# Units four to seven load into the weights' staging tiles, the third job's splits move behind unit seven's places, and 32 dummy matmuls go

## The chip, the cores and the metric

The kernel runs on one core of one Trainium2 chip. The metric is the device time of one execution in microseconds (us). The core has five engines that each take their own instructions in order: PE (matmuls and transposes), DVE (elementwise, scans and reductions), ACT (activations and copies), POOL (here the scatters) and SP (here only DMA issues). ACT and POOL issue DMAs too, and an issue stands in the engine's order like any other instruction.

## The reference

Two parts follow each other. A gated scan runs over 4 sequences of 3648 steps with 256 channels: with z the gate's logits and lower bound lb,

```python
sig = 1.0 / (1.0 + np.exp(-f_logit))
f = lb + (1.0 - lb) * sig
h = f[:, t] * h + (1.0 - f[:, t]) * x[:, t]      # for every step t
```

Then each of the 14592 rows of h goes through a mixture of 16 experts: a router gives 4 group logits and 4 x 4 expert logits, the largest of each picks one expert per row, and the row's result is `combined * (relu(h @ w1[e]) @ w2[e])` with w1 256 x 1024, w2 1024 x 256, and `combined` the product of the two softmax weights that were picked. All is in float32.

## The kernel before, in words

**Units.** The rows are taken in units of 512, counted from 0 (units 0 to 28, the last one half full). Unit u's z and x (1 MB together) are loaded into one `zt` tile (p1_load; four buffers). ACT makes the tanh (L195) and two affine steps (L205), which together are the gate f; DVE multiplies by the gate (L241, from unit 10 on L221; in this text "the gate" of the unit) and runs two scans, one per half of the channels (L232). PE transposes h back to rows (L259) and multiplies by the router's weights (L278). ACT copies these (rs, L283), PE transposes them (L291), ACT copies the logits (Lg, L292). DVE's routing of the unit begins with mx (L301, a maximum over Lg) and ends with posi (L398), the place of each row in its expert's list; between them lie PE's counts (L383 to L386) and small steps on DVE. POOL then scatters the unit's rows to these places in DRAM (L361, four scatters per unit). Units 0 to 7 are routed one by one; from unit 8 on two units are routed together (GROUPS).

**Jobs.** While units are still under way, experts whose list has enough rows are begun: job i takes its first rows once the units below EARLY[i][0] are scattered (4, 6, 8, 8, 10, ...), 256 rows for the first four jobs. SP loads the rows (xr, L852) after the last scatter of those units has landed; PE transposes them (L933), ACT and DVE make the operands. Jobs 0 and 1 multiply in float32 (L967, then L1002) and need no split of the weights. From job 2, "the third job", the weights are loaded into staging tiles `st` (eight of 512 KB), ACT casts them to f16 (wh, L878) and DVE makes the remainder (wl, L879), four of each per job; then come three matmuls for each product (L989 to L991, L1019). After the early jobs, sixteen more take the rest of each expert's list.

**What sets the order.** SP goes in the order in which the program is written. On PE, DVE, ACT and POOL a scheduler moves instructions within the dependences and its own estimates; on every engine the order is then fixed. Loads up to unit 11 stand on SP, later ones on ACT (ZX_SP). In before, p1_load of units u+2 and u+3 is called while unit u is worked on (`range(u + AHEAD - 1, u + FAR)`). A load into a `zt` buffer waits for the scans of the unit that had the buffer. Dummy matmuls (keep_warm, L268) run before each raw job's row transposes, 22 each.

Of the kernel before, what the change touches and what calls it, by code (L numbers as in the profile page):

```python
# [10 lines left out]
F32 = mybir.dt.float32  # L11
# [7 lines left out]
P = 128  # L19
# [18 lines left out]
O_BUFS = 5  # L38
X_BUFS = 4
AHEAD = 3  # L40
FAR = 4
BEGIN = 6
MT = -(-max(CAPS) // 128)
QUARTERS = (13, 14, 15)
ZX_SP = 12
# [3 lines left out]
def gated_scan_moe(ctx: ExitStack, tc, zx, lower, wroute, wexp, out, S):  # L49
# [116 lines left out]
        at += g  # L166
    assert at == NU
    last_load = {}

    def p1_load(u):  # L170
        if u >= NU or u in units:
            return
        a, b = unit_range(u)
        w = b - a
        zt = p1.tile([P, 2, KD, UNIT], F32, name="zt", bufs=4)
        src = zx[u * P:(u + 1) * P, :].rearrange("p (s k w) -> p s k w", s=2, k=KD)
        if u == 0:
            for k in range(KD):
                for q in range(2):
                    nc.sync.dma_start(out=zt[:, q, k, 0:w], in_=src[:, q, k, 0:w])  # L180
        elif u == 1:
            for k in range(KD):
                nc.sync.dma_start(out=zt[:, :, k, 0:w], in_=src[:, :, k, 0:w])
        else:
            last_load[u] = (nc.sync if u < ZX_SP else nc.scalar).dma_start(out=zt[:, :, :, 0:w], in_=src[:, :, :, 0:w])
        units[u] = {"z": zt}

    def p1_tanh(u):
        a, b = unit_range(u)
        w = b - a  # L190
        U = units[u]
        U["h"] = p1.tile([P, KD, UNIT], F32, name="h", bufs=3)
        U["f"] = ff = U["z"][:, 0]
        if u > 1:
            nc.scalar.activation(ff[:, :, 0:w], U["z"][:, 0, :, 0:w], AF.Tanh, scale=0.5)  # L195

    def p1_affine(u):
        a, b = unit_range(u)
        w = b - a
        U = units[u]  # L200
        ff = U["f"]
        for k in range(KD):
            if u <= 1:
                nc.scalar.activation(ff[:, k, 0:w], U["z"][:, 0, k, 0:w], AF.Tanh, scale=0.5)
            nc.scalar.activation(ff[:, k, 0:w], ff[:, k, 0:w], AF.Identity, scale=hlf[:, k:k + 1],  # L205
                                 bias=cen[:, k:k + 1])

# [4 lines left out]
    def p1_tb(u, k):  # L212
        a, b = unit_range(u)
        w = b - a
        U = units[u]
        ff = U["f"]
        h = U["h"]
        U["u"] = U["z"][:, 1]
        if (k == 0 or u <= 1) and "gated" not in U:
            ks = slice(k, k + 1) if u <= 1 else slice(0, KD)  # L220
            nc.vector.scalar_tensor_tensor(out=U["u"][:, ks, 0:w], in0=ff[:, ks, 0:w], scalar=1.0,  # L221
                                           in1=U["z"][:, 1, ks, 0:w], op0=ALU.subtract, op1=ALU.mult)
        uu = U["u"]
        cuts = [a] + [c for c in range(0, N, S) if a < c < b] + [b]
        for c0, c1 in zip(cuts[:-1], cuts[1:]):
            if c0 % S == 0:
                init = 0.0
            elif c0 > a:
                init = h[:, k, c0 - a - 1:c0 - a]
            else:  # L230
                init = units[u - 1]["h"][:, k, UNIT - 1:UNIT]
            nc.vector.tensor_tensor_scan(out=h[:, k, c0 - a:c1 - a], data0=ff[:, k, c0 - a:c1 - a],  # L232
                                         data1=uu[:, k, c0 - a:c1 - a], initial=init,
                                         op0=ALU.mult, op1=ALU.subtract)

    def p1_gate(u):
        a, b = unit_range(u)
        w = b - a
        U = units[u]
        U["gated"] = True  # L240
        nc.vector.scalar_tensor_tensor(out=U["z"][:, 1, :, 0:w], in0=U["f"][:, :, 0:w], scalar=1.0,  # L241
                                       in1=U["z"][:, 1, :, 0:w], op0=ALU.subtract, op1=ALU.mult)

    def p1_back(u, i):
        a, b = unit_range(u)
# [40 lines left out]
    def p1_logits(u, Lg, pos):  # L286
        a, b = unit_range(u)
        nt = (b - a) // P
        rs = units[u]["rs"]
        lt = bank("p")  # L290
        nc.tensor.transpose(out=lt[:, 0:32 * nt], in_=rs[0:32 * nt, 0:P], identity=ident[0:32 * nt, 0:32 * nt])  # L291
        nc.scalar.copy(Lg[:, pos:pos + nt, :], lt[:, 0:32 * nt].rearrange("p (t c) -> p t c", c=32)[:, :, 0:20])  # L292

    def route_thunks(G, T, fast=False):
        V = nc.vector
# [97 lines left out]
        def f5():  # L393
# [1 line left out]
            sc = rt.tile([P, T, NE], F32, name="sc", bufs=1)  # L395
            V.tensor_tensor(out=sc, in0=pv[:, 0:T], in1=R["oh16"], op=ALU.mult)
            posi = R["posi"] = rt.tile([P, T], I32, name="posi", bufs=4)
            V.tensor_reduce(out=posi, in_=sc, axis=AX, op=ALU.add)  # L398
            new = state["runoff"] = rt.tile([P, NE], F32, name="runoff")
            nc.scalar.copy(new, pv[:, T])  # L400

# [5 lines left out]
    def p1_thunks(us, groups, parts):  # L407
# [53 lines left out]
        for u in us + [us[-1] + 1]:  # L461
            seq = []
            if u <= FAST:
                put(lambda u=u: [p1_load(v) for v in range(u + AHEAD - 1, u + FAR)])
                ending = u - 1 in ends
                if not ending:
                    put(lambda u=u: p1_ta(u + 1))
# [405 lines left out]
    def job_split(j, i):  # L873
# [2 lines left out]
        j.wh[i] = wp.tile([P, 1024], F16, name=f"wh{i}")  # L876
        j.wl[i] = wp.tile([P, 1024], BF16, name=f"wl{i}")
        nc.scalar.copy(j.wh[i], j.st[i])  # L878
        nc.vector.tensor_tensor(out=j.wl[i], in0=j.st[i], in1=j.wh[i], op=ALU.subtract)  # L879

    def job_xt(j, pi):
        b0, rows = j.pieces[pi]
        ch = max(i for i, (a, _) in enumerate(j.chunks) if a <= b0)
        c0 = b0 - j.chunks[ch][0]
        if j.raw:
            keep_warm(bank("m2"), 22)
            j.xh[ch] = mo.tile([P, 2 * P], F32, name="xh", bufs=X_BUFS)
            j.xl[ch] = mo.tile([P, 2 * P], F32, name="xl", bufs=X_BUFS)
        elif c0 == 0:
# [360 lines left out]
```

## Time and profile before

| | |
|---|---|
| median of 3 runs | 773.15 us (770.84 to 774.26) |
| profiled execution | 771.69 us, of which the span from the first to the last instruction is 769.8 us |
| mean granted PE clock in the span | 0.981 of full speed |
| busy | PE 720.2 us (94%), DVE 537.2 (70%), ACT 453.3 (59%), POOL 296.7 (39%) |

The profiled execution lies 1.46 us under the median. In a timeline a row gives the start, the duration, engine, line, operation and tile (written <- read), and in brackets the engine's idle time just before it with what ended that. "ACTq" and "SPq" are issues of DMAs on that engine's queue; the transfer itself goes on afterwards. Consecutive instructions of one kind make one row (x8 is eight of them).

### The profile page before, as it was taken

To read this page: it belongs to the slowest core of one execution; us is meant where nothing else is said; L and a number is where in the kernel's file an instruction comes from. 1 tells how busy PE (TensorE), PEld (TensorE's weight loads), DVE (VectorE), ACT (ScalarE), POOL (GpSimd) and SP (SyncE) were. 2 spreads that over 40 slices of the span, in tenths; PEclk is the share of its full clock that TensorE was granted. 3 is DMA by queue.
4 is the path that set the end of the run, shared out by engine and by line. 5 is a ranking of instruction groups with operands and counts; after the bars stand their busy time and mean duration, and the time that the engine had idled before them with its cause. 6 is when DMAs were issued, how large, how long until landed. Compare 5 with 4: busy or idle time off the path is not lost.

```text
span 769.8 us, 21533 instructions
## 1 busy us (share of the span) xinstructions
PE 720.2 (94%) x8179; PEld 640.4 (83%) x8179; DVE 537.2 (70%) x1166; ACT 453.3 (59%) x827; POOL 296.7 (39%) x272
## 2 busy tenths in 40 slices
PE   3668798999999999999999999999999999999995
PEld 1456587988888888898999889999999999999895
DVE  6997669999999986687546545453754675667561
ACT  5647768887787865545545444444544565556551
POOL 3653255587765576441221212222222222223232
PEclk9969899999999999999999999999999999999998
DMA  7799689989888866448875662424254455556530
GB/s 279 223 388 347 211 318 319 358 263 306 324 299 270 261 219 192 124 114 245 197 187 151 149 138 83 125 77 128 92 157 110 142 153 154 155 170 194 165 83 29
DMA packets 101961, 152.02 MB, mean 197 GB/s; under 512 B 60962, under 2 KB 70977, under 8 KB 98528
## 3 DMA queue, kind: packets, MB, share of 16 engines
q1 hardware_dynamic: 87328, 103.27, 46.1%
q0 software_dynamic: 11408, 30.02, 10.8%
q10 hardware_dynamic: 3120, 17.34, 6.6%
q8 instruction: 64, 1.05, 0.6%
q14 instruction: 41, 0.34, 0.1%
HBM read 112.66 MB, written 38.40 MB: 196 GB/s over the span
## 4 chain that ended last, share of the span: by engine, by line
PE 64%; DVE 12%; DMA 9%; issue 6%; ACT 5%; POOL 2%; SPq 1%; POOLq 0%; ACTq 0%; DVEq 0%
PE ps_m L1019 30%; PE ps_m L989 7%; PE ps_m L990 7%; PE ps_m L991 7%; DMA xs<-rows,posi 4%; PE ps_p L989 3%; PE ps_p L991 3%; PE ps_p L990 3%; DVE h L232 3%; DVE wl L879 2%; DMA zt<-in_zx_dram 2%; PE ps_p L259 2%; DMA xs<-blank 2%; POOL out_dram L1032 1%; DVE hl L995 1%
## 5 line engine op out<-in xcount | busy, mean ns | idle before, releaser
L1019 PE MATMUL ps_m<-wh,hh 128*128 128x256 f16 (+3 forms) x1256 | 254.7, 251 | 1.5 <-ACT o L1031 1.5
L1019 PE MATMUL ps_m<-wh,hl 128*128 128x256 f16 (+3 forms) x1256 | 254.9, 251 | 0.1
L1019 PE MATMUL ps_m<-wl,hh 128*128 128x256 bf16 (+3 forms) x1256 | 254.6, 251 | 0.0
L1019 PEld LDWEIGHTS <-hh 128*128 128x128 f16 (+3 forms) x2512 | 186.3, 99 | 23.3 <-issue 4.8
L989 PE MATMUL ps_m<-xh,wh 128*128 128x256 f16 (+12 forms) x798 | 191.9, 255 | 6.1 <-DVE hl L995 5.6
L990 PE MATMUL ps_m<-xl,wh 128*128 128x256 bf16 (+12 forms) x798 | 192.0, 255 | 0.0
L991 PE MATMUL ps_m<-xh,wl 128*128 128x256 f16 (+12 forms) x798 | 192.0, 255 | 0.0
L361 POOL DMA_INDIRECT xs<-rows,posi x114 | 144.2, 1265 | 104.4 <-issue 28.6
L879 DVE TENSOR_TENSOR wl<-st,wh 128x1024 bf16<-128x1024 f32 x120 | 144.6, 1218 | 51.5 <-ACT wh L878 51.0
L1032 POOL DMA_INDIRECT out_dram<-o,info x71 | 82.8, 1166 | 235.8 <-ACT o L1031 203.0
L995 DVE SCALAR_TENSOR_TENSOR hl<-ps_m,hh 128x512 bf16<-128x512 f32 (+10 forms) x170 | 112.8, 667 | 61.4 <-ACT hh L994 61.1
L994 ACT ACTIVATE hh<-ps_m 128x512 f16<-128x512 f32 (+10 forms) x170 | 99.4, 588 | 66.4 <-PE ps_m L991 64.7
L878 ACT CAST wh<-st 128x1024 f16<-128x1024 f32 x120 | 124.2, 1049 | 13.5 <-PE ps_m L1019 8.9
L990 PEld LDWEIGHTS <-wh 128*128 128x128 f16 x1104 | 108.2, 98 | 13.1 <-issue 6.0
L989 PEld LDWEIGHTS <-wh 128*128 128x128 f16 x1104 | 108.1, 98 | 8.9 <-issue 1.2
L991 PEld LDWEIGHTS <-wl 128*128 128x128 bf16 x1104 | 108.2, 98 | 7.0
L1019 PEld LDWEIGHTS <-hl 128*128 128x128 bf16 (+3 forms) x1256 | 99.3, 99 | 10.0 <-issue 0.4
L1032 POOL DMA_INDIRECT out_dram<-o,meta x53 | 60.6, 1143 | 106.1 <-ACT o L1031 87.0
L1031 ACT ACTIVATE o<-ps_m,info 128x256 f32<-128x256 f32 (+4 forms) x71 | 31.4, 444 | 76.2 <-PE ps_m L1019 68.8
L989 PE MATMUL ps_p<-xh,wh 128*128 128x256 f16 (+17 forms) x306 | 71.5, 249 | 0.0
L990 PE MATMUL ps_p<-xl,wh 128*128 128x256 bf16 (+17 forms) x306 | 71.5, 249 | 0.0
L991 PE MATMUL ps_p<-xh,wl 128*128 128x256 f16 (+17 forms) x306 | 71.5, 249 | 0.0
(183 smaller groups left out, 837.6 us busy)
## 6 DMA issues: line engine op xcount, KB each, us to landing
st<-in_wexp_dram SPq DMA_DIRECT2D x120, 512.0 KB
zt<-in_zx_dram ACTq DMA_DIRECT2D x16, 1024.0 KB
zt<-in_zx_dram SPq DMA_DIRECT2D x10, 1024.0 KB
xs<-blank SPq DMA_DIRECT2D x28, 258.0 KB
xr<-xs SPq DMA_DIRECT2D x14, 258.0 KB
wh<-in_wexp_dram SPq DMA_DIRECT2D x8, 256.0 KB
wl<-in_wexp_dram SPq DMA_DIRECT2D x8, 256.0 KB
xs<-rows,posi POOLq DMA_INDIRECT x114, 6.7
```

The lines of the kernel that those rows point to most:

```text
L232: nc.vector.tensor_tensor_scan(out=h[:, k, c0 - a:c1 - a], data0=ff[:, k, c0 - a:c1 - a], data1=uu[:, k, c0 - a:c1 - a], initial=init, op0 ...
L361: sc = nc.gpsimd.indirect_dma_start(out=xs_v[G["t0"] + t][:, :], out_offset=bass.IndirectOffsetOnAxis(ap=R["posi"][:, t:t + 1], axis=0), i ...
L878: nc.scalar.copy(j.wh[i], j.st[i])
L879: nc.vector.tensor_tensor(out=j.wl[i], in0=j.st[i], in1=j.wh[i], op=ALU.subtract)
L989: nc.tensor.matmul(po, w1_at(j.wh, k, c), xh[:, k], start=(k == 0), stop=False)
L990: nc.tensor.matmul(po, w1_at(j.wh, k, c), xl[:, k], start=False, stop=False)
L991: nc.tensor.matmul(po, w1_at(j.wl, k, c), xh[:, k], start=False, stop=(k == KD - 1))
L994: nc.scalar.activation(hi, pv, AF.Relu)
L995: nc.vector.scalar_tensor_tensor(out=j.hl[ch][:, cs[0]:cs[-1] + 1, 0:w], in0=pv, scalar=0.0, in1=hi, op0=ALU.max, op1=ALU.subtract)
L1019: nc.tensor.matmul(pm[i * q:i * q + n, 0:dw], h[ch][:, c, ts], w2_at(w, c)[:, i * dw:(i + 1) * dw], start=(c == 0 and s == 0), stop=(c == ...
L1031: nc.scalar.activation(o[s, 0:dw], pm[s, 0:dw], AF.Copy, scale=lt.bitcast(F32)[s, r, 1:2])
L1032: nc.gpsimd.indirect_dma_start(out=out_v[out_n[0]].rearrange("n (g d) -> (n g) d", g=g), out_offset=bass.IndirectOffsetOnAxis(ap=lt[s, r, ...
```

## The change: what it does

Four parts. (1) Units 4 to 7 no longer use `zt`: z and x are loaded as two transfers of 512 KB into two staging tiles each, all eight issued on SP right after the loads of units 2 and 3. The `zt` buffers of units 0, 1 and 2 so go to units 8, 9 and 10, whose loads follow directly, and that of unit 3 to unit 11. The loads of one early unit u are now called for all v in range(2, min(8 + u, 12)); from unit 12 on the load is called by unit u + 2's own step alone, on ACT. (2) The third job's four wl splits are held behind the posi of unit 7. (3) The dummies before job 0 go from 22 to 12, those before job 1 from 22 to none. (4) A unit's z and x are named apart in the code, which changes no instruction.

```diff
@@ -38,8 +38,9 @@
 O_BUFS = 5
 X_BUFS = 4
 AHEAD = 3
-FAR = 4
+STAGED = range(4, 8)
 BEGIN = 6
+BEHIND = {2: 7}
 MT = -(-max(CAPS) // 128)
 QUARTERS = (13, 14, 15)
 ZX_SP = 12
@@ -166,14 +167,24 @@
         at += g
     assert at == NU
     last_load = {}
+    loaded = set()
 
     def p1_load(u):
-        if u >= NU or u in units:
+        if u >= NU or u in loaded:
             return
+        loaded.add(u)
         a, b = unit_range(u)
         w = b - a
+        src = zx[u * P:(u + 1) * P, :].rearrange("p (s k w) -> p s k w", s=2, k=KD)
+        if u in STAGED:
+            halves = []
+            for q in range(2):
+                t = stg.tile([P, 1024], F32, name="st").rearrange("p (k w) -> p k w", k=KD)
+                nc.sync.dma_start(out=t[:, :, 0:w], in_=src[:, q, :, 0:w])
+                halves.append(t)
+            units[u] = {"z": halves[0], "x": halves[1]}
+            return
         zt = p1.tile([P, 2, KD, UNIT], F32, name="zt", bufs=4)
-        src = zx[u * P:(u + 1) * P, :].rearrange("p (s k w) -> p s k w", s=2, k=KD)
         if u == 0:
             for k in range(KD):
                 for q in range(2):
@@ -183,16 +194,16 @@
                 nc.sync.dma_start(out=zt[:, :, k, 0:w], in_=src[:, :, k, 0:w])
         else:
             last_load[u] = (nc.sync if u < ZX_SP else nc.scalar).dma_start(out=zt[:, :, :, 0:w], in_=src[:, :, :, 0:w])
-        units[u] = {"z": zt}
+        units[u] = {"z": zt[:, 0], "x": zt[:, 1]}
 
     def p1_tanh(u):
         a, b = unit_range(u)
         w = b - a
         U = units[u]
         U["h"] = p1.tile([P, KD, UNIT], F32, name="h", bufs=3)
-        U["f"] = ff = U["z"][:, 0]
+        U["f"] = ff = U["z"]
         if u > 1:
-            nc.scalar.activation(ff[:, :, 0:w], U["z"][:, 0, :, 0:w], AF.Tanh, scale=0.5)
+            nc.scalar.activation(ff[:, :, 0:w], U["z"][:, :, 0:w], AF.Tanh, scale=0.5)
 
     def p1_affine(u):
         a, b = unit_range(u)
@@ -201,7 +212,7 @@
         ff = U["f"]
         for k in range(KD):
             if u <= 1:
-                nc.scalar.activation(ff[:, k, 0:w], U["z"][:, 0, k, 0:w], AF.Tanh, scale=0.5)
+                nc.scalar.activation(ff[:, k, 0:w], U["z"][:, k, 0:w], AF.Tanh, scale=0.5)
             nc.scalar.activation(ff[:, k, 0:w], ff[:, k, 0:w], AF.Identity, scale=hlf[:, k:k + 1],
                                  bias=cen[:, k:k + 1])
 
@@ -215,11 +226,11 @@
         U = units[u]
         ff = U["f"]
         h = U["h"]
-        U["u"] = U["z"][:, 1]
+        U["u"] = U["x"]
         if (k == 0 or u <= 1) and "gated" not in U:
             ks = slice(k, k + 1) if u <= 1 else slice(0, KD)
             nc.vector.scalar_tensor_tensor(out=U["u"][:, ks, 0:w], in0=ff[:, ks, 0:w], scalar=1.0,
-                                           in1=U["z"][:, 1, ks, 0:w], op0=ALU.subtract, op1=ALU.mult)
+                                           in1=U["x"][:, ks, 0:w], op0=ALU.subtract, op1=ALU.mult)
         uu = U["u"]
         cuts = [a] + [c for c in range(0, N, S) if a < c < b] + [b]
         for c0, c1 in zip(cuts[:-1], cuts[1:]):
@@ -238,8 +249,8 @@
         w = b - a
         U = units[u]
         U["gated"] = True
-        nc.vector.scalar_tensor_tensor(out=U["z"][:, 1, :, 0:w], in0=U["f"][:, :, 0:w], scalar=1.0,
-                                       in1=U["z"][:, 1, :, 0:w], op0=ALU.subtract, op1=ALU.mult)
+        nc.vector.scalar_tensor_tensor(out=U["x"][:, :, 0:w], in0=U["f"][:, :, 0:w], scalar=1.0,
+                                       in1=U["x"][:, :, 0:w], op0=ALU.subtract, op1=ALU.mult)
 
     def p1_back(u, i):
         a, b = unit_range(u)
@@ -291,6 +302,8 @@
         nc.tensor.transpose(out=lt[:, 0:32 * nt], in_=rs[0:32 * nt, 0:P], identity=ident[0:32 * nt, 0:32 * nt])
         nc.scalar.copy(Lg[:, pos:pos + nt, :], lt[:, 0:32 * nt].rearrange("p (t c) -> p t c", c=32)[:, :, 0:20])
 
+    placed = {}
+
     def route_thunks(G, T, fast=False):
         V = nc.vector
         R = {}
@@ -395,7 +408,7 @@
             sc = rt.tile([P, T, NE], F32, name="sc", bufs=1)
             V.tensor_tensor(out=sc, in0=pv[:, 0:T], in1=R["oh16"], op=ALU.mult)
             posi = R["posi"] = rt.tile([P, T], I32, name="posi", bufs=4)
-            V.tensor_reduce(out=posi, in_=sc, axis=AX, op=ALU.add)
+            placed[G["t0"]] = V.tensor_reduce(out=posi, in_=sc, axis=AX, op=ALU.add).ins
             new = state["runoff"] = rt.tile([P, NE], F32, name="runoff")
             nc.scalar.copy(new, pv[:, T])
 
@@ -461,7 +474,7 @@
         for u in us + [us[-1] + 1]:
             seq = []
             if u <= FAST:
-                put(lambda u=u: [p1_load(v) for v in range(u + AHEAD - 1, u + FAR)])
+                put(lambda u=u: [p1_load(v) for v in range(2, min(8 + u, ZX_SP))])
                 ending = u - 1 in ends
                 if not ending:
                     put(lambda u=u: p1_ta(u + 1))
@@ -876,14 +889,16 @@
         j.wh[i] = wp.tile([P, 1024], F16, name=f"wh{i}")
         j.wl[i] = wp.tile([P, 1024], BF16, name=f"wl{i}")
         nc.scalar.copy(j.wh[i], j.st[i])
-        nc.vector.tensor_tensor(out=j.wl[i], in0=j.st[i], in1=j.wh[i], op=ALU.subtract)
+        with tc.issue_after(placed[BEHIND[j.idx] * 4]) if j.kind == "A" and j.idx in BEHIND else ExitStack():
+            nc.vector.tensor_tensor(out=j.wl[i], in0=j.st[i], in1=j.wh[i], op=ALU.subtract)
 
     def job_xt(j, pi):
         b0, rows = j.pieces[pi]
         ch = max(i for i, (a, _) in enumerate(j.chunks) if a <= b0)
         c0 = b0 - j.chunks[ch][0]
         if j.raw:
-            keep_warm(bank("m2"), 22)
+            if j.idx == 0:
+                keep_warm(bank("m2"), 12)
             j.xh[ch] = mo.tile([P, 2 * P], F32, name="xh", bufs=X_BUFS)
             j.xl[ch] = mo.tile([P, 2 * P], F32, name="xl", bufs=X_BUFS)
         elif c0 == 0:
```

On ACT the load of unit 12 and the tanh stand as follows. In before, from the tanh of unit 8 on (xh and xl are job 0's row operands, rs and Lg those of unit 6, the second tanh is unit 9's):

```order
L195 ACTIVATE zt<-zt 128x1024
L205 ACTIVATE zt<-zt,mid,half 128x512 x2
L939 COPY xh<-ps_p 128x256
L939 COPY xl<-ps_p 128x256
L283 COPY rs<-ps_p 128x128
L292 COPY Lg<-ps_p 128x80
L195 ACTIVATE zt<-zt 128x1024
```

And after, from the tanh of unit 11 on; the DMA is unit 12's load, the second tanh unit 12's:

```order
L206 ACTIVATE zt<-zt 128x1024
L216 ACTIVATE zt<-zt,mid,half 128x512 x2
L196 DMA zt<-in_zx_dram 128x2048
L206 ACTIVATE zt<-zt 128x1024
L954 COPY xh<-ps_p 128x256
L954 COPY xl<-ps_p 128x256
L294 COPY rs<-ps_p 128x128
L216 ACTIVATE zt<-zt,mid,half 128x512 x2
L303 COPY Lg<-ps_p 128x80
```

Job 0's operands and unit 6's logits stood behind the tanh of unit 8, whose load is on SP; they now stand behind the tanh of unit 12, whose load is issued one row ahead of it. In before the same load stood 22 rows of the order below job 0's xh, and its tanh another 22 rows below it.

On DVE, around the routing of unit 6, before (from unit 7's last scan; the gate and the two scans of 128x512 are unit 8's, mx and what follows are unit 6's routing):

```order
L232 SCALAR_TENSOR_TENSOR h<-zt 128x448
L241 SCALAR_TENSOR_TENSOR zt<-zt 128x1024
L232 SCALAR_TENSOR_TENSOR h<-zt,h 128x512
L301 TENSOR_REDUCE mx<-Lg 128x20
L232 SCALAR_TENSOR_TENSOR h<-zt,h 128x512
L303 TENSOR_TENSOR ge<-Lg,mx 128x80
L307 SCALAR_TENSOR_TENSOR pw<-ge,pri 128x80
```

And after, from unit 7's last scan; the scans of 128x512 are unit 8's (two) and unit 9's (two), and `zt<-zt` x2 are the gates of units 11 and 12:

```order
L243 SCALAR_TENSOR_TENSOR h<-st 128x448
L243 SCALAR_TENSOR_TENSOR h<-zt,h 128x512 x2
L232 SCALAR_TENSOR_TENSOR zt<-zt 128x1024 x2
L314 TENSOR_REDUCE mx<-Lg 128x20
L243 SCALAR_TENSOR_TENSOR h<-zt,h 128x512
L316 TENSOR_TENSOR ge<-Lg,mx 128x80
L243 SCALAR_TENSOR_TENSOR h<-zt,h 128x512
L320 SCALAR_TENSOR_TENSOR pw<-ge,pri 128x80
```

The gate of unit 8 is gone from here (it, and those of units 9 and 10, now stand among the routing of units 4 and 5), and two gates that stood far behind unit 7's places now stand ahead of unit 6's mx.

Also on DVE, the end of unit 7's routing and the third job's splits (wl), before:

```order
L309 TENSOR_REDUCE pm<-pw 128x20
L879 TENSOR_TENSOR wl_1263<-st,wh_1262 128x1024
L311 TENSOR_TENSOR oh<-pw,pm 128x80
L879 TENSOR_TENSOR wl_1271<-st,wh_1270 128x1024
L372 TENSOR_TENSOR oh16f<-oh 128x64
L335 SCALAR_TENSOR_TENSOR se<-sm,oh 128x16
L879 TENSOR_TENSOR wl_1316<-st,wh_1315 128x1024
L338 TENSOR_REDUCE s_1123<-se 128x4
L396 TENSOR_TENSOR sc<-ps_p,oh16f 128x64
L340 SCALAR_TENSOR_TENSOR s_1125<-sm,s_1123 128x4
L879 TENSOR_TENSOR wl_1322<-st,wh_1321 128x1024
```

And after, from unit 7's posi on:

```order
L411 TENSOR_REDUCE posi<-sc 128x4
L356 RECIPROCAL rows<-s_1100 128x4
L893 TENSOR_TENSOR wl_1236<-st,wh_1235 128x1024
L628 SCALAR_TENSOR_TENSOR posA<-runoff,taken 128x16
L604 SCALAR_TENSOR_TENSOR fill<-runoff,least 128x16
L893 TENSOR_TENSOR wl_1244<-st,wh_1243 128x1024
```

All four splits left the stretch between unit 7's mx and its posi and follow it.

## Rows read from the trace of the kernel before

**Rows 1.** The page: span, and busy time of each engine.
```profile
span 769.8 us, 21533 instructions
PE 720.2 (94%) x8179; PEld 640.4 (83%) x8179; DVE 537.2 (70%) x1166; ACT 453.3 (59%) x827; POOL 296.7 (39%) x272
```
**Rows 2.** Windows: length, busy PE PEld DVE ACT POOL, PEclk, DMA share, GB/s.
```profile
90.00:100.00 10.00, 5.41 (x31) 3.94 (x32) 5.17 (x12) 3.77 (x9) 0.00 (x0) 0.66 0.94 329
...
60.95:101.24 40.29, 33.55 (x227) 26.92 (x227) 27.85 (x62) 25.95 (x54) 8.07 (x8) 0.92 0.82 282
...
140.00:250.00 110.00, 107.94 (x1146) 95.23 (x1144) 108.54 (x241) 87.29 (x166) 72.67 (x55) 1.00 0.90 302
```
**Rows 3.** The chain that ended last, 0 to 140 us: start, us, what.
```profile
2.62 6.29 DMA zt<-in_zx_dram
...
49.81 8.20 DMA zt<-in_zx_dram
...
83.48 4.87 DMA xs<-rows,posi
...
89.25 5.76 DMA xr<-xs
```
**Rows 4.** Timeline of DVE, 60 to 78 us.
```profile
60.68 1.23 DVE L241 SCALAR_TENSOR_TENSOR zt<-zt 128x1024 f32<-128x1024 f32 x1 [2.08 <-ACT zt L205]
62.01 1.28 DVE L232 TENSOR_TENSOR_SCAN h<-zt,h 128x512 f32<-128x512 f32 x1
63.21 0.21 DVE L301 TENSOR_REDUCE mx<-Lg 128x20 f32<-128x80 f32 x1
...
66.92 0.22 DVE L398 TENSOR_REDUCE posi<-sc 128x4 int32<-128x64 f32 x1 [0.37 <-DVE rows L343]
68.28 1.22 DVE L241 SCALAR_TENSOR_TENSOR zt<-zt 128x1024 f32<-128x1024 f32 x1 [1.14 <-ACT zt L205]
...
72.51 1.21 DVE L879 TENSOR_TENSOR wl<-st,wh 128x1024 bf16<-128x1024 f32 x1
...
77.79 0.19 DVE L398 TENSOR_REDUCE posi<-sc 128x4 int32<-128x64 f32 x1
```
**Rows 5.** Timeline of ACT, 58 to 73 us.
```profile
58.03 1.06 ACT L195 ACTIVATE zt<-zt 128x1024 f32<-128x1024 f32 x1 [2.81 <-DMA zt<-in_zx_dram]
59.12 1.52 ACT L205 ACTIVATE zt<-zt,mid,half 128x512 f32<-128x512 f32 x2
60.55 0.35 ACT L939 COPY xh<-ps_p 128x256 f32<-128x256 f32 x1
...
72.85 0.33 ACTq L185 DMA_DIRECT2D zt<-in_zx_dram  x1
```
**Rows 6.** Timeline of PE, 54 to 102 us.
```profile
54.23 4.20 PE L268 MATMUL ps_m<-upto,tri 128*128 128x128 bf16 x44
...
60.95 0.70 PE L967 MATMUL ps_m<-xh,wh 128*128 128x256 f32 x2 [0.64 <-ACT xh L939]
...
93.48 0.46 PE L933 MATMUL ps_p<-ident,xr 128*128 128x128 f32 x1 [3.95 <-DMA xr<-xs]
95.05 0.92 PE L933 MATMUL ps_p<-ident,xr 128*128 128x128 f32 x3 [1.12 <-DMA xr<-xs]
...
96.91 1.22 PE L967 MATMUL ps_m<-xh,wl 128*128 128x256 f32 x2
...
98.64 0.60 PE L967 MATMUL ps_m<-xh,wl 128*128 128x256 f32 x2
...
101.24 0.38 PE L989 MATMUL ps_m<-xh,wh 128*128 128x256 f16 x2
```
**Rows 7.** Timeline of POOL: unit 7's first and last of four scatters.
```profile
79.65 0.97 POOL L361 DMA_INDIRECT xs<-rows,posi  x1 [6.70 <-ACT runoff L400]
...
83.48 1.03 POOL L361 DMA_INDIRECT xs<-rows,posi  x1 [0.30 <-issue]
```
**Rows 8.** Waits of PE, 101 to 360 us: us in total, times, longest.
```profile
PE ps_m L989 <- DVE hl L995: 5.6, 7, 1.7
```

## The prediction

> **What bounds the kernel now.** I read the page first. PE is busy 720.2 of 769.8 us, 94% [rows 1], so in most stretches PE is the bound, and only stretches where PE stands still or runs slowly can give or take anything. The windows then show where that is: from 60.95 us (the first matmul of job 0) to 101.24 us (the first of the third job) PE is busy 33.55 of 40.29 us, so 6.74 us idle, and in the slice from 90 to 100 us the granted clock is 0.66, between its levels of 1.2 and 2.4 GHz [rows 2]. PE's timeline names the reason: 3.95 us and 1.12 us of waiting for the third job's rows (xr), and after that wait the work goes at half speed, a pair of job 0's matmuls taking 1.22 us at 96.91 and 0.60 at 98.64 [rows 6]. About 4.0 us are worked at the slow level (0.46 us, and 95.05 to 98.64), so some 1.9 us are lost there. The chain of waits says what made the rows late: unit 7's last scatter starts at 83.48 and lands 4.87 us on, the load of the rows takes 5.76 more [rows 3]; earlier in the same chain stands the load of unit 8, issued at 49.81 and landing 8.20 us later. ACT stood 2.81 us for it [rows 5], and DVE 2.08 us for unit 8's gate [rows 4]. So the change works on what the chain ran through: a load that comes late, and four splits of 1.21 us on DVE ahead of unit 7's places [rows 4].
>
> **The change part by part.** The question is when PE can begin job 0 (60.95 before), when the third job's rows come, and what PE does in between.
>
> *Loads ahead.* Units 4 to 10 are all asked for before the first jobs' weights, so nothing waits for unit 8 any more: DVE's 2.08 us go. But the gates of units 8, 9 and 10 now stand ahead of unit 6's routing. At 1.22 us [rows 4] they cost at most 3 x 1.22 = 3.7 us, at least nothing, if they fall into short waits of the routing of units 4 and 5. That routing is one step after the other on DVE, so I take 3.7. DVE was free for unit 8 at 60.68 - 2.08 = 58.60; now it is at 62.3, and unit 8's two scans of 1.28 us end at 64.9. Before, they ended at 64.6 (62.01 and two scans). What the load gave, the gates take back.
>
> *Unit 12's load.* This is the part that decides. The load is the first that ACT issues, it goes into unit 8's buffer, so it can't be issued before unit 8's second scan ends, at 64.9. Before, it was issued at 72.85, but nothing stood directly behind it [rows 5]. Now the tanh of unit 12 does, the next row on ACT, and behind that job 0's xh and xl, unit 6's rs and Lg, and on DVE the gate of unit 12 ahead of unit 6's mx. So the first job and the routing wait for a transfer of 1 MB. Loads of this size or less took 6.29 and 8.20 us [rows 3]; the third job's weights (2 MB) are asked for at about the same time. I keep both ends: it lands at 71.2 to 73.1. The tanh takes 1.06, xh 0.35 [rows 5], so PE begins job 0 at 72.6 to 74.5, that is 11.7 to 13.6 us late. In this part of the program the queues carry 282 GB/s at a busy share of 0.82 [rows 2], so the load isn't alone on them.
>
> The Trainium skill ("DMA: Bandwidth & Descriptors", section "Issuing engines are not separate DMA queues") says that transfers issued by different engines share the same 16 DMA engines and interleave, so moving a load to ACT's queue buys no bandwidth; the two landings above, 6.29 and 8.20 us for 1 MB or less, agree. Its section "Anatomy of one DMA" gives 2.0 us plus the bytes at 436 GB/s, by which I estimate 4.4 us for this load, and the sum below would be +0.2 us instead of +3.1.
>
> *Routing of units 6 and 7.* After the tanh (72.3 to 74.2) ACT makes xh and xl, rs and the two affine steps (1.52 us), in all some 2.4 us; unit 12's gate follows (1.22), so unit 6's mx stands at 75.9 to 77.8, where it was at 63.21 [rows 4]. From there to unit 7's posi it was 77.79 - 63.21 = 14.6 us. The four splits (4.8 us), unit 9's gate (1.22) and its wait (1.14) are no longer in it, so 7.4 us remain and posi(7) comes at 83.3 to 85.2, 5.5 to 7.4 us later than before. The splits now follow it; they are needed only by the third job's first products, after its rows, so they cost nothing there.
>
> *Scatters.* The eight of units 6 and 7 now come nearly in one row. Four take 83.48 - 79.65 = 3.8 us from the first start to the last [rows 7], so 1.28 each. By unit 7's posi, with the same 1.7 us before the first scatter, the last one starts at 89.0 to 90.9; by POOL, seven steps (9.0 us) behind unit 6's posi, which ends 3.9 us after its mx begins [rows 4], so at 79.8 to 81.7, it is 88.8 to 90.7, the same. Before, 95.05 - 83.48 = 11.57 us lay from that start to PE having the rows. So the third job's rows are there at 100.6 to 102.5, where they were at 95.05.
>
> *What PE does meanwhile.* Now PE has both raw jobs in front of it from 72.6 to 74.5 on. What it did from 60.95 to 101.24 is 33.55 - 1.9 = 31.6 us at full clock, so it is busy until 104 to 106: it no longer waits for the rows, and the 6.74 us idle and the 1.9 us at half clock go. Against that PE stands nearly idle for more than ten us before job 0 begins, as it did before 95.05, and the first products will run at the lower level. Between no loss and the 1.9 us that the same situation cost at 95.05, I take 1.9, the nearest row.
>
> *Dummies.* 32 of 44 go, 4.20 us x 32/44 = 3.1 us of PE [rows 6]. They lay in a stretch where PE waits for ACT's xh anyway (0.64 us idle behind them); with job 0 starting 12 us later their place is idle. Worth 0 to -0.6 us; I take 0. Their other use, holding the clock, is in the 1.9 above.
>
> *Sum.* Up to the third job's first matmul: +11.7 to +13.6 (late start), -6.74 (idle gone), -1.9 (half clock gone), +1.9 (half clock at job 0) = +5.0 to +6.9, middle +5.9. Later, PE waits 5.6 us from 101 to 360 us for DVE's hl [rows 8], in a stretch where DVE itself is full (108.54 of 110 us, [rows 2]); a PE that is later by six us finds DVE further ahead. Between nothing and 5.6 given back no row is nearer, I take the middle, 2.8. So +3.1 on the profiled execution: 771.69 + 3.1 = 774.8. The median of the runs lies 1.46 us higher, so I forecast 776.3 us. With the low ends (shorter landing, all 5.6 back, the gates hidden in part) this case reaches down to 772, with nothing given back up to 780.
>
> **The rivals.**
> *Faster.* The change does what its parts suggest: unit 8's wait (2.08) and the splits (4 x 1.15 net = 4.6) leave the path to unit 7's places, the third job's rows come 6.7 us earlier, and PE's 3.95 + 1.12 us of waiting and the 1.9 us at half clock go: -7.0, so 766.2 on the median's footing. For it speaks that the chain of before runs through exactly these rows. Against it, that ACT's order puts unit 12's tanh, with its load one row ahead, in front of job 0's operands and unit 6's logits. It decides if job 0 still begins by about 62.6, since PE has 31.6 us to do ahead of the third job (62.6 + 31.6 = 94.2, which is 7.0 before 101.24), and that needs a load of unit 12 for which ACT hardly waits.
>
> *The wait is short.* With a landing as short as the 4.87 us of the smallest transfer in rows 3, job 0 starts 2.4 us earlier than the middle above: +0.7, so 773.9, no change.
>
> *Worse.* Unit 13's load has the same form: its tanh stands seven rows behind it on ACT, and job 1's relu outputs behind that. If a landing of 8.20 us is covered only by half, 4 us more are lost: 780.3. Against it, PE has job 0's second product (some 7 us) for that time.
>
> **How the numbers follow.** The forecast's case gets 0.55, faster 0.20, the short wait 0.10, worse 0.15. About 0.5%, or 3.9 us, is what a measurement of this kernel can tell from no change; the forecast of +3.1 lies just below it. I split its 0.55 into 0.27 slower and 0.28 the same: within its own range, 772 to 780, the bound lies near the middle. With the worse case slower is 0.42, with the short wait the same is 0.38, and faster 0.20. The range, 767 to 783, holds the forecast's case and the short wait, nearly all of the worse case and the slower half of the faster one.
>
> **What would show it.** Right: ACT idle for 6 us or more ahead of an L206, ended by a `zt` load; PE's first L982 (job 0) after 70 us; mx of unit 6 after 74; the scatters of units 6 and 7 in one row of eight; no wait of PE for xr in front of the third job, and its first product (L1004) at 104 to 108. Wrong: job 0 beginning near 61 us, since then nothing is late and the faster case holds; or PE idle again ahead of the third job, since then the rows came later than worked out; or a start of the third job late by six us or more and yet the same end, since then more was given back than the 5.6 us of rows 8.

## The result, and the profile after

The changed kernel takes 782.63 us (median of 4 runs, 778.32 to 784.08) against 773.63 us (4 runs): a ratio of 1.0114, interval 1.0067 to 1.0161. Run once more beside the kernel before, it is 1.0125 (1.0098 to 1.0151). So it is slower by 1.1 to 1.3 per cent, some 9 us. The forecast was 776.3, slower by 0.4 per cent, with a range up to 783: the sign is right, the size that was forecast is a third of what was measured.

The page of the changed kernel, first the span, then busy time by engine, as in [rows 1]:

```profile
span 780.8 us, 21459 instructions
PE 718.8 (92%) x8147; PEld 637.2 (82%) x8147; DVE 536.8 (69%) x1166; ACT 456.0 (58%) x827; POOL 296.1 (38%) x272
```

PE has the same work, less 32 dummies, and 11 us more span. Where it fell behind is read from the windows of both kernels: after the stretch and its length comes PE's busy time. First before, then the changed one:

```profile
0.00:60.00 60.00, 34.04 (x287) 25.43 (x290) 48.54 (x159) 35.75 (x73) 30.96 (x54) 0.89 0.84 301
60.00:80.00 20.00, 17.69 (x119) 14.40 (x113) 16.04 (x42) 13.76 (x29) 5.14 (x6) 1.00 0.98 338
80.00:100.00 20.00, 14.93 (x113) 11.48 (x112) 12.09 (x22) 13.14 (x28) 3.59 (x4) 0.83 0.67 221
100.00:120.00 20.00, 19.44 (x166) 16.16 (x165) 15.81 (x35) 15.74 (x31) 13.64 (x10) 1.00 0.89 324
120.00:200.00 80.00, 77.30 (x837) 67.81 (x835) 79.08 (x183) 63.32 (x123) 52.57 (x40) 0.98 0.93 313
```

```profile
0.00:60.00 60.00, 28.92 (x240) 20.43 (x241) 50.30 (x161) 42.64 (x82) 31.87 (x52) 0.80 0.93 336
60.00:80.00 20.00, 9.05 (x46) 5.94 (x49) 7.83 (x11) 6.17 (x14) 2.59 (x3) 0.50 0.64 204
80.00:100.00 20.00, 18.95 (x149) 15.24 (x141) 18.81 (x50) 13.51 (x32) 9.41 (x8) 0.99 0.60 170
100.00:120.00 20.00, 15.06 (x98) 11.97 (x102) 9.29 (x28) 8.39 (x17) 4.39 (x4) 0.83 0.78 275
120.00:200.00 80.00, 79.68 (x848) 70.11 (x837) 77.79 (x169) 65.62 (x125) 52.76 (x42) 1.00 0.95 311
```

A kernel's busy time of the whole span less that of the windows so far is what PE still has to do. By that the changed kernel is behind by 3.7 us at 60 (689.9 against 686.2), 12.3 at 80, 8.3 at 100, 12.7 at 120 and 10.3 at 200; its span ends 11.0 us later. So it loses up to 80 us, makes good 4 us while the kernel before waits for its third job's rows, loses as much again in a wait of its own from 100 on, and gets back some two. Where the 3.7 us up to 60 come from isn't taken apart here.

ACT's timeline shows the first loss (compare [rows 5]):

```profile
57.66 1.07 ACT L206 ACTIVATE zt<-zt 128x1024 f32<-128x1024 f32 x1
58.76 1.52 ACT L216 ACTIVATE zt<-zt,mid,half 128x512 f32<-128x512 f32 x2
63.52 0.33 ACTq L196 DMA_DIRECT2D zt<-in_zx_dram  x1
71.91 1.06 ACT L206 ACTIVATE zt<-zt 128x1024 f32<-128x1024 f32 x1 [11.63 <-DMA zt<-in_zx_dram]
72.88 0.35 ACT L954 COPY xh<-ps_p 128x256 f32<-128x256 f32 x1
```

ACT is done with unit 11 at 60.28, stands until unit 8's scans let unit 12's load go at 63.52, and then 8.39 us more until it has landed. Behind it stand job 0's xh and, on DVE, unit 12's gate and unit 6's mx (compare [rows 4]):

```profile
63.41 1.20 DVE L232 SCALAR_TENSOR_TENSOR zt<-zt 128x1024 f32<-128x1024 f32 x1
75.11 1.23 DVE L232 SCALAR_TENSOR_TENSOR zt<-zt 128x1024 f32<-128x1024 f32 x1 [10.50 <-ACT zt L216]
76.25 0.23 DVE L314 TENSOR_REDUCE mx<-Lg 128x20 f32<-128x80 f32 x1
78.15 1.28 DVE L243 TENSOR_TENSOR_SCAN h<-zt,h 128x512 f32<-128x512 f32 x1 [1.67 <-PE ps_p L270]
...
83.11 0.21 DVE L411 TENSOR_REDUCE posi<-sc 128x4 int32<-128x64 f32 x1
...
85.60 0.22 DVE L411 TENSOR_REDUCE posi<-sc 128x4 int32<-128x64 f32 x1
```

The second loss is in PE's timeline (compare [rows 6]; L948 are the third job's row transposes, L1004 its first products):

```profile
73.28 1.22 PE L982 MATMUL ps_m<-xh,wh 128*128 128x256 f32 x2 [10.95 <-ACT xh L954]
...
98.36 0.59 PE L982 MATMUL ps_m<-xl,wl 128*128 128x256 f32 x2
104.94 1.22 PE L948 MATMUL ps_p<-ident,xr 128*128 128x128 f32 x4 [5.99 <-DMA xr<-xs]
...
114.87 1.03 PE L1017 MATMUL ps_m<-wh,hh 128*128 128x256 f32 x4
...
118.32 0.27 PE L1004 MATMUL ps_m<-xh,wh 128*128 128x256 f16 x1
```

Job 0 begins 12.3 us late. PE then works through, but stops at 98.95, and the third job's rows stand next in its order: 5.99 us idle, and the transposes and what follows run at half speed. Work of the raw jobs (jobs 0 and 1, which multiply in float32) that needs no rows stands behind them: 26 matmuls of their second products (L1017, here the four at 114.87), where in the kernel before 6 stood between the transposes and the third job's first product. That first product comes at 118.32, 17.1 us later than before. The chain of waits of the changed kernel, start, us and what, says why the rows are late (compare [rows 3]):

```profile
93.70 8.65 DMA xs<-rows,posi
...
102.69 2.11 DMA xr<-xs
```

The last scatter starts 10.2 us later than before, and that is the whole lateness of the rows. Its landing is longer, 8.65 us instead of 4.87 (unit 14's load, issued on ACT at 95.15, is under way beside it), but the load of the rows behind it is shorter by as much, 2.11 instead of 5.76: from the scatter's start to PE having the rows it is 11.24 us, before 11.57.

### The profile page after: what moved, and what is told of

It reads as the page before. It is cut to its first block, busy times and chain, and to the rows that moved or that the text cites. A ratio compares the mean times of both kernels' runs of the same rounds, so it can differ in the third digit from the quotient of the medians.

```text
span 780.8 us, 21459 instructions
## 1 busy us (share of the span) xinstructions
PE 718.8 (92%) x8147; PEld 637.2 (82%) x8147; DVE 536.8 (69%) x1166; ACT 456.0 (58%) x827; POOL 296.1 (38%) x272
## 4 chain that ended last, share of the span: by engine, by line
PE 62%; DVE 12%; issue 5%; DMA 4%; POOL 2%; SPq 2%; ACT 1%; POOLq 0%; DVEq 0%; ACTq 0%
PE ps_m L1034 29%; PE ps_m L1004 7%; PE ps_m L1006 6%; PE ps_m L1005 6%; PE ps_p L1004 3%; PE ps_p L1005 3%; PE ps_p L1006 3%; DVE wl L893 3%; DVE hl L1010 2%; DVE h L243 2%; DMA xs<-rows,posi 2%; PE ps_m L1017 2%; DMA xs<-blank 2%; PE ps_p L270 1%; DVE zt L232 1%
## 5 line engine op out<-in xcount | busy, mean ns | idle before, releaser
L1004 PE MATMUL ps_m<-xh,wh 128*128 128x256 f16 (+12 forms) x798 | 191.8, 255 | 5.3 <-DVE hl L1010 5.3
L374 POOL DMA_INDIRECT xs<-rows,posi x114 | 142.1, 1246 | 128.7 <-issue 26.5
L1004 PEld LDWEIGHTS <-wh 128*128 128x128 f16 x1104 | 107.9, 98 | 10.1 <-issue 1.6
L1047 POOL DMA_INDIRECT out_dram<-o,meta x53 | 62.2, 1174 | 113.5 <-ACT o L1046 95.1
L1004 PE MATMUL ps_p<-xh,wh 128*128 128x256 f16 (+17 forms) x306 | 71.6, 250 | 0.0
```

What stands on the lines that cost most here:

```text
L374: sc = nc.gpsimd.indirect_dma_start(out=xs_v[G["t0"] + t][:, :], out_offset=bass.IndirectOffsetOnAxis(ap=R["posi"][:, t:t + 1], axis=0), i ...
L1004: nc.tensor.matmul(po, w1_at(j.wh, k, c), xh[:, k], start=(k == 0), stop=False)
L1047: nc.gpsimd.indirect_dma_start(out=out_v[out_n[0]].rearrange("n (g d) -> (n g) d", g=g), out_offset=bass.IndirectOffsetOnAxis(ap=lt[s, r, ...
```

## The experiments

The theories: A, the wait for unit 12's load ahead of job 0 and of unit 6's routing costs the time. B, the missing dummies and the clock do. C, the moved splits do. D, after A, PE loses because the rows' transposes stand ahead of raw work. E, the rows' lateness itself is the cost wherever they stand. The diffs are against the changed kernel, where nothing else is said. In the first group of runs (the first four below) every kernel took some 7 per cent longer, the kernel before 826.28 us, with PE standing still for nothing the profile names; so only ratios to the kernel before of the same group are compared, and times that the expectations give in us are not met there.

**The loads of before, with the other parts.**
```diff
-STAGED = range(4, 8)
+STAGED = ()
-                put(lambda u=u: [p1_load(v) for v in range(2, min(8 + u, ZX_SP))])
+                put(lambda u=u: [p1_load(v) for v in range(u + AHEAD - 1, u + 4)])
```


> The loads of before (units 4 to 7 in zt, look-ahead of before), with the third job's splits behind unit 7's places and 12 dummies. If the load of unit 12 ahead of job 0's operands is what costs (theory A), job 0 begins near 61 us again, unit 7's places come up to 4.6 us earlier, and the kernel takes 766 to 772 us. If the missing dummies and the clock are what costs (theory B), it stays at 776 or more with half clock from 61 us on. If the moved splits cost (theory C), 776 or more with PE waiting for wl at the third job.

Measured: 1.0004 (0.9971 to 1.0037). Job 0 begins at 62.73, and PE doesn't wait for the third job's rows. Without the staging the loss is gone, so it lies in the loads; with 12 dummies job 0's first pairs take 1.22 us, twice the full speed's 0.59.

**Without the hold on the splits.**
```diff
-BEHIND = {2: 7}
+BEHIND = {}
```


> The changed kernel without the hold on the third job's splits. Theory A: ACT still waits some 11 us for unit 12's load, 780 to 787 us. Theory C: back to 773 to 777 us. Theory B says nothing new: 780 to 784.

Measured: 1.0179 (1.0098 to 1.0261). ACT waits 11.12 us for unit 12's load as in the changed kernel. C is out: without the moved splits it is no faster.

**The dummies of before.**
```diff
-            if j.idx == 0:
-                keep_warm(bank("m2"), 12)
+            keep_warm(bank("m2"), 22)
```


> The changed kernel with 22 dummy matmuls ahead of each raw job again. Theory A: they stand some 12 us before job 0's first product, so 780 to 784 us, job 0 at about 73 us. Theory B: clock full in 73 to 80 us, 773 to 778 us.

Measured: 1.012 (1.0065 to 1.0174). PE's timeline of this kernel:

```profile
60.07 3.43 PE L279 MATMUL ps_m<-upto,tri 128*128 128x128 bf16 x44
...
76.66 1.22 PE L981 MATMUL ps_m<-xh,wh 128*128 128x256 f32 x2 [10.89 <-ACT xh L953]
```

The 44 dummies end 13 us before job 0 begins, and its first pair takes 1.22 us all the same. B is out as the cause of this loss, as long as job 0 begins that late; what the dummies are worth when it begins near 60 us is seen in the last experiments.

**Unit 12's load and tanh held, and the gates of units 11 and 12.** On ACT both are queued behind unit 7's runoff copy (L413, the running counts per expert that the next unit starts from), on DVE the gates behind unit 7's posi (the replaced lines, and the one that sets `placed["act"]`, are left out):
```diff
+            with tc.issue_after(placed["act"]) if u == 12 else ExitStack():
                 last_load[u] = (nc.sync if u < ZX_SP else nc.scalar).dma_start(...)
...
+            with tc.issue_after(placed["act"]) if u == 12 else ExitStack():
                 nc.scalar.activation(ff[:, :, 0:w], U["z"][:, :, 0:w], AF.Tanh, scale=0.5)
...
+            with tc.issue_after(placed[28]) if u in (11, 12) else ExitStack():
                 nc.vector.scalar_tensor_tensor(out=U["u"][:, ks, 0:w], ...)
```


> The changed kernel with unit 12's load and tanh queued on ACT behind unit 7's runoff copy, and the gates of units 11 and 12 queued on DVE behind unit 7's places; nothing else. Theory A: ACT no longer waits ahead of job 0's operands, job 0 begins at 61 to 63 us, unit 7's places come at about 72, the third job's rows at about 88 to 90, and the kernel takes 764 to 770 us, less than before. Theory B: the half clock stays and it takes 776 or more. Theory C: 776 or more, with waits for wl.

Measured: 1.0039 (1.0017 to 1.0061), against 1.012 and 1.0179 of its neighbours that keep the wait. Most of the loss is gone, as A has it, but no gain: less than A promised. The gates of units 11 and 12 moved with the load, so the two are not told apart.

**Before and after again, for a group without that disturbance.**

> The kernel before again, for a trace on the chip of this group. If the chip of the first group only adds time of its own from 140 us on (PE waiting with nothing to wait for), the first 120 us look as on the first chip: job 0 at 61 to 63 us, the third job's first product at 100 to 102.

Measured: one run of 774.82 us; job 0 at 62.10, PE waits 3.32 and 1.43 us for the third job's rows, and the third job's first product comes at 102.39, nearly as at first.

> The changed kernel again, beside the others of this group: 1.01 to 1.015 of before.

Measured: 1.0125 (1.0098 to 1.0151); job 0 at 73.61, the wait for the rows 5.07 us.

**The third job's transposes behind job 0's second products on PE.**
```diff
+            if j.kind == "A" and j.idx == 2:
+                break
             th.append(lambda pi=pi: job_xt(j, pi))
...
+        if mi == 1:
+            with tc.issue_after(placed["raw2"]):
+                for pi in range(len(macros[2][0].pieces)):
+                    job_xt(macros[2][0], pi)
```


> The changed kernel with the third job's row transposes behind job 0's second products on PE; nothing else is meant to move. If their place ahead of some 8 us of raw work is what left PE idle 6 us and at half clock for 6 us (theory D), that wait is filled: no idle time over 2 us ahead of them, and 6 to 8 us less than the changed kernel, 0.991 to 0.993 of it. If the rows' lateness itself is the cost (theory E), the third job's first product comes no earlier than in the changed kernel and the time is within 2 us of it.

Measured: 1.0163 (1.0135 to 1.0192), no gain. PE's timeline, then ACT's:

```profile
106.38 1.03 PE L1017 MATMUL ps_m<-wl,hl 128*128 128x256 f32 x4
111.46 1.13 PE L948 MATMUL ps_p<-ident,xr 128*128 128x128 f32 x4 [4.05 <-ACT Lg L303]
```
```profile
109.75 1.04 ACT L891 CAST wh<-st 128x1024 f16<-128x1024 f32 x1 [9.93 <-DMA st<-in_wexp_dram]
```

PE now works on to 107.4, where it stopped at 98.95, and then waits for ACT, which stands 9.93 us at a cast of the fourth job's weights. SP asks for these behind the third job's rows, so they are late for the same reason as the rows. The order moved on ACT too, so this run alone doesn't settle D.

**The same, with the fourth job's casts held behind the third job's xh on ACT.**
```diff
...
+        with tc.issue_after(placed["xh", "A", 2]) if j.kind == "A" and j.idx == 3 else ExitStack():
             nc.scalar.copy(j.wh[i], j.st[i])
```


> e6 with the fourth job's casts held behind the third job's xh on ACT, so that ACT doesn't stand at weights that have not come. Theory D: the wait ahead of the third job's row transposes is under 1 us now and the kernel takes 1.003 to 1.008 of before, 5 to 7 us less than the changed kernel (1.0125). Theory E: 1.010 or more, the wait goes to another place.

Measured: 1.0178 (1.0123 to 1.0234). PE's waits from 60 to 125 us, in us, times and longest:

```profile
PE ps_m L984 <- ACT xh L955: 12.6, 1, 12.6
PE ps_m L1006 <- ACT xh L958: 2.7, 1, 2.7
PE ps_p L270 <- ACT rows L272: 1.1, 1, 1.1
```

No wait for the rows is left, and the kernel is no faster: PE is idle 3.2 us from 140 to 200 us, where the changed kernel is idle 0.3. That is one wait, for DVE's routing of later units (scn). First this kernel, then the changed one:

```profile
152.91 0.19 PE L339 MATMUL ps_p<-scn,tri 128*128 128x16 bf16 x1 [3.20 <-DVE scn L332]
```
```profile
152.76 0.19 PE L339 MATMUL ps_p<-scn,tri 128*128 128x16 bf16 x1 [0.32 <-DVE scn L332]
```

PE is there some 2.7 us earlier and goes on at the same time. In the kernel before, the same step (L326) stands at 142.03, 10.7 us earlier, which is nearly the whole loss. So D is out as a way to win the time: by then DVE's routing is as late as PE, and PE meets it. That agrees with E, which says only that the rows' lateness is the cost wherever they stand; that DVE, which stood still 10.50 us for unit 12's gate, carries the lateness on its own isn't tested alone.

**Part 2 alone.**
```diff
-STAGED = range(4, 8)
+STAGED = ()
-            if j.idx == 0:
-                keep_warm(bank("m2"), 12)
+            keep_warm(bank("m2"), 22)
...
```
(the loads as in the first experiment)

> The kernel before with part 2 alone: the third job's splits behind unit 7's places; loads and the 44 dummies as before. Theory A: the splits leave unit 7's routing, the third job's rows come 3 to 5 us earlier, PE no longer waits 5 us for them, 0.991 to 0.996 of before. Theory C (the moved splits cost): 1.00 or more, with PE waiting for wl.

Measured: 764.6 us, 0.9925 (0.9897 to 0.9953), faster than both kernels. PE's timeline and the chain of waits of this kernel:

```profile
60.80 0.70 PE L981 MATMUL ps_m<-xh,wh 128*128 128x256 f32 x2 [0.64 <-ACT xh L953]
...
88.85 1.00 PE L947 MATMUL ps_p<-ident,xr 128*128 128x128 f32 x4
```
```profile
83.47 2.56 DMA xs<-rows,posi
...
86.93 2.25 DMA xr<-xs
```

PE has the rows at 88.85 instead of 95.05 and doesn't wait. But not as expected: unit 7's posi is 4.0 us earlier (73.82) and its last scatter is not (83.47 against 83.48 in [rows 7]). The scatters do not wait for the places, but for ACT's copy of unit 7's rows, in both kernels. In before the chain says so (L261), in this kernel POOL's timeline (L272):

```profile
75.47 2.26 PE ps_m L1002 x10
...
78.88 0.49 ACT rows L261
...
79.65 0.34 POOL xs L361
```
```profile
79.64 0.97 POOL L374 DMA_INDIRECT xs<-rows,posi  x1 [6.83 <-ACT rows L272]
```

That copy needs PE's transposes of unit 7, which stand behind job 0's second products on PE at 78.03 us in both. What became shorter are the landings, 2.56 and 2.25 us against 4.87 and 5.76 [rows 3]. Transfers beside them moved: the two blank transfers (SP's, which fill rows of xs with a blank row) are issued at 78.90 instead of 81.11, and unit 13's load (88.62 on ACT) follows the rows' load (86.37) instead of standing beside it. That these make the difference is read from the traces; no run moves them alone. For the scatter it isn't even clear in the trace: in before the DMA engines carry nothing from 86 to 88 us (the last two figures are DMA share and GB/s), while its landing is signalled only at 88.35.

```profile
86.00:88.00 2.00, 2.00 (x21) 1.69 (x12) 0.76 (x2) 2.00 (x6) 0.00 (x0) 1.00 0.00 0
```

This kernel differs from that of the first experiment only in having 44 dummies where that has 12: 0.9925 against 1.0004, though in two groups of runs, the first of them the disturbed one.

**The hold of the first group again.**

> The hold of e5 once more (unit 12's load and tanh behind unit 7's runoff copy, gates of units 11 and 12 behind unit 7's places), on whatever chip this group gets. Theory A on a chip like the first: job 0 at 62 to 66 us, 0.992 to 1.000 of before, that is 1.2 to 2 per cent less than the changed kernel (1.0125). If it stays above 1.005 there, the wait for unit 12's load is not what the change costs.

Measured: 1.0051 (1.0019 to 1.0083), job 0 at 61.03. Beside the changed kernel's 1.0125 (from the group before, on another chip) the wait for unit 12's load, with the two gates, is worth some 0.7 per cent, less than expected; the kernel is still slower than before, and by the bound that was set, 1.005, A just misses: the wait is a part of the cost, not all of it.

**All gates held, 44 dummies.** Added to the last: the gates of units 8, 9 and 10 behind the posi of units 5, 6 and 7, and the dummies of before.
```diff
+        with tc.issue_after(placed[4 * (u - 3)]) if u in (8, 9) else ExitStack():
             nc.vector.scalar_tensor_tensor(out=U["x"][:, :, 0:w], in0=U["f"][:, :, 0:w], ...)
...
-            with tc.issue_after(placed[28]) if u in (11, 12) else ExitStack():
+            with tc.issue_after(placed[28]) if u in (10, 11, 12) else ExitStack():
...
-            if j.idx == 0:
-                keep_warm(bank("m2"), 12)
+            keep_warm(bank("m2"), 22)
```


> The hold of e9, and the gates of units 8, 9 and 10 behind the places of units 5, 6 and 7 as well, with the 44 dummies of before: the loads come early, but nothing of what they make possible is done ahead of the routing. If the three gates ahead of the routing cost their 3.7 us and no more, unit 7's places come 2 to 4 us earlier than in e9 and it takes 0.984 to 0.993 of before, below e8 (0.9925). If loading ahead itself delays the first units, it is not below e8.

Measured: 764.4 us, 0.994 (0.9916 to 0.9964). DVE's timeline around unit 7's posi, first of the hold before, then of this kernel:

```profile
70.99 0.24 DVE L317 TENSOR_REDUCE mx<-Lg 128x20 f32<-128x80 f32 x1 [2.62 <-ACT Lg L306]
73.33 0.22 DVE L414 TENSOR_REDUCE posi<-sc 128x4 int32<-128x64 f32 x1
```
```profile
68.25 0.21 DVE L318 TENSOR_REDUCE mx<-Lg 128x20 f32<-128x80 f32 x1
70.50 0.22 DVE L415 TENSOR_REDUCE posi<-sc 128x4 int32<-128x64 f32 x1
```

Unit 7's places come 2.8 us earlier and the third job's rows 4.4 us (88.02 against 92.38 on PE). But the staging, with the side effects that were named held off, is no better than part 2 alone (0.9925): the early loads gain nothing that can be measured.

**The same with 12 dummies.** The last step, its dummies as in the changed kernel.

> e10 with the 12 dummies of the changed kernel in place of 44, nothing else. It takes apart what e9 and e10 differ in (1.0051 and 0.994). If the three gates ahead of the routing made the difference, 0.992 to 0.996 of before; if the dummies made it, by the clock at job 0's start, 1.002 to 1.006.

Measured: 0.999 (0.9962 to 1.0018), between the two expectations. So of the 1.1 per cent between the last two, the gates make some 0.6 and the dummies some 0.5, each to within some 0.4, and this run was on another chip than those two. PE of this kernel runs job 0's first pair at half speed and yet has the third job's transposes at the same time:

```profile
59.03 1.22 PE L988 MATMUL ps_m<-xh,wh 128*128 128x256 f32 x2
...
88.02 0.46 PE L954 MATMUL ps_p<-ident,xr 128*128 128x128 f32 x1 [3.68 <-DMA xr<-xs]
```
```profile
59.19 0.70 PE L987 MATMUL ps_m<-xh,wh 128*128 128x256 f32 x2
...
88.02 0.46 PE L953 MATMUL ps_p<-ident,xr 128*128 128x128 f32 x1 [3.73 <-DMA xr<-xs]
```
(first with 12 dummies, then with 44). PE's remaining busy time differs by 1.8 us at 100, 2.5 at 200 and 4.3 at 360 us, so most of the difference comes up later, where the order of the instructions differs as well. Whether the clock or that order makes it stays open. Taken together, the changed kernel stands 2.0 per cent above part 2 alone, and the three steps (the wait with its gates 0.7, the gates of units 8 to 10 0.6, the dummies 0.5) make up nearly all of it: the change gains with part 2 and loses more with part 1, and what part 3 costs shows only once job 0 begins early again.

## Why the prediction was right or wrong

*Loads ahead.* Right in kind, the size too high: unit 8's scans end at 63.49 (61.06 and 2.43 for the two), where 64.9 was taken for three gates in full and 61.2 for none. The gates, with whatever else moved ahead of these scans, cost 2.3 us there.

*Unit 12's load.* Right. It was issued at 63.52 and took 8.39 us to the tanh, a little over the upper end of 8.20; job 0 began at 73.28 (72.6 to 74.5 said), unit 6's mx stood at 76.25 (75.9 to 77.8). That this is a good half of the loss is shown: held, together with the gates of units 11 and 12, it is worth 0.7 of 1.25 per cent. One reading beside it was wrong: of the third job's weights only 1 MB was asked for ahead of this load, at 62.27; the other 1 MB followed at 72.02, after it had landed.

*Routing of units 6 and 7.* Somewhat off: the posi of unit 7 ended at 85.8 (83.3 to 85.2 said), that of unit 6 at 83.3 (79.8 to 81.7), since 1.67 us of waiting for PE's transposes and both scans of unit 9 fell into it; before there was one scan between unit 6's mx and posi.

*Scatters.* The eight run in one row from 84.10 to 95.6, the last beginning at 93.70 (89.0 to 90.9 said), because the first waits for unit 6's later posi. From there to PE having the rows 11.57 us were taken and 11.24 measured, but by luck: the scatter's landing was 8.65 instead of 4.87 us, the rows' 2.11 instead of 5.76. PE had the rows at 104.94, not at 100.6 to 102.5.

*What PE does meanwhile.* This is the step that failed. "It no longer waits for the rows, and the 6.74 us idle and the 1.9 us at half clock go" took the work between 60.95 and 101.24 as work that PE could do ahead of the rows. But its part from 95.05 on, 6.2 us, stood behind the transposes in PE's order before, and in the changed kernel 20 more matmuls of the raw jobs' second products (L1017) do. PE ran out at 98.95, not at 104 to 106, the rows came 6 us later, and both items of the sum that were struck out came back: 5.99 us idle and again half speed from 104.94 to about 111, some 3 us. With these two the sum of +5.9 at the third job becomes about +15; measured at its first product it is +17.1 (118.32 against 101.24); the rest is, by estimate, more half clock at job 0 and other work that now stands ahead. By PE's remaining work, which leaves the order out, it is 12.7 at 120 us. The two runs that put the transposes last show that this time isn't simply to be had by another order, though: the wait then goes to ACT, which stands at weights that SP asks for behind the rows, and with that held off to DVE's routing.

*Half clock at job 0.* Taken as 1.9 us; the pairs run at 1.22 to 1.06 us from 73.28 to 79.8, so it was about 3.

*Given back.* The size is near, 2.8 us taken and 2.4 measured (from 12.7 at 120 to 10.3 at 200), but the mechanism was wrong. It was to come from PE's waits for DVE's hl, 5.6 us before [rows 8], with DVE further ahead. In the changed kernel, from 118 to 371 us, they are nearly what they were:

```profile
PE ps_m L1004 <- DVE hl L1010: 5.3, 4, 2.5
```

DVE was not further ahead: it had stood for unit 12's load as well, busy 7.83 us from 60 to 80 where it was busy 16.04 before.

*The rule that was weighed.* The estimate after the Trainium skill's "DMA: Bandwidth & Descriptors" (section "Anatomy of one DMA"), 4.4 us for 1 MB, was half of the measured 8.39 us, with 1 MB of weights asked for just ahead of it; that section gives its figures for transfers that POOL issues, and this load is issued on ACT. By its section "Issuing engines are not separate DMA queues" a load gains no bandwidth on another engine's queue, and the measured times agree: 8.39 us for unit 12's load on ACT, 8.20 for unit 8's on SP before. (The two landings named in the prediction are both of loads on SP, so they couldn't tell.) The rows' load fits too: 5.76 us on SP with unit 13's load issued on ACT beside it, 2.25 with that load behind it.

*The rivals.* The faster case fell with ACT's order, as said. Its price was about right for part 2 alone, -7.0 us said, 771.22 to 764.6 measured, but the rows came earlier by shorter landings and not by earlier places, which the scatters did not wait for. The worse case, unit 13's load, did not happen: ACT waited 0.71 us for it. The time came out near the worse case's 780.3, by another mechanism, and that it still lies within the range, by 0.4 us, is luck.

*The signs.* Of those for right, ACT's wait (11.63 us), job 0 after 70, mx after 74 and the eight scatters in a row came; no wait for xr and a first product at 104 to 108 did not. Of those for wrong, one came: PE idle again ahead of the third job.

## What to carry to other kernels

When a load and its first use stand side by side in an in-order queue, everything behind them waits for the landing; a load that comes earlier can free a buffer earlier and so let the scheduler place a later load and its use at the front of a queue, ahead of work on the critical path. In a sum, idle time may be struck out only against work that stands ahead of the wait in the engine's own order. A later PE finds DVE ahead only if DVE wasn't held up by the same wait. And the landing time of a small transfer on the chain is not a constant: it went from 2.56 to 8.65 us here, with other transfers beside it each time, though no run shows that these alone made it.

## What was not expected of the hardware

The same scatter of unit 7's last rows landed in 2.56, 4.87 and 8.65 us in three kernels, and the load of the third job's rows in 2.25, 5.76 and 2.11 us, without a change in their size; in before the scatter was signalled as landed at 88.35 us, though the DMA engines carried nothing from 86 to 88 us. And in the first group of runs the kernel before took 826.28 us, on the chip where it took 771.22 us in the second; the trace of the first experiment shows PE busy 232 of 260 us from 140 to 400 us with a granted clock of 0.93, where part 2 alone, in the second group, shows 255 us and 1.00. What held PE up there, the profile doesn't name.
